# Cross network on one core: the first weights' queue, the products that start the clock, and a lag in the last layer's sums

## The chip, the cores and the metric

The kernel runs on one core of one Trainium2 chip. The metric is device time in microseconds (us) of one execution. A profile is one more execution, recorded by the hardware profiler; its "span" starts at the first instruction of the core, and all times of profiles below count from there.

The tables in plain fences below are worked out from the records of those traces (when each of the 16 DMA engines reported a landing, when a packet or an instruction started, when the granted TensorE clock changed).

## The reference

```python
B, F, D, L = 16384, 26, 16, 6
Din = min(F * D, 1024)                 # 416
def reference(x0, ws, bs):             # x0 (16384, 416), ws (6, 416, 416), bs (6, 416), bf16
    x = x0
    for l in range(6):
        proj = jnp.einsum('bd,de->be', x, ws[l]) + bs[l]
        x = x0 * proj + x
    return x
```

## The kernel before

The features lie on the partitions (three tiles of 128 and one of 32), the 16384 rows on the free axis, in eight groups of 2048 rows, a group in four chunks of 512. PE multiplies, ACT takes the products out of PSUM and adds the bias, DVE multiplies by x0 and adds x. Groups and layers are interleaved so that PE always has a tile to go on with. SP issues nearly all transfers.

The first group is loaded as rows and transposed on PE, the others by transposing transfers. The head of the program, with the transfers of the first group (`load_nat`), the first weights (`load_wm(0, ...)`) and the products that only keep PE busy:

```python
    load_wm(0, "act")                      # first weights, 312 KB, on ACT's queue
    load_nat(0, 0, 2)                      # first chunk of rows, first half, on SP's queue
    load_nat(0, 2, KK)                     # second half
    for j in range(1, NJ):
        load_nat(j, 0, KK)                 # chunks 2 to 4, 416 KB each
    load_w3(0, "sp")
    load_group(1, lambda: load_wm(1, "sp"))
    ...
    def keep_busy(n, b):
        for _ in range(n):
            add("pe", lambda h: h.matmul(bank(b, n=P), ident[:, :], ident[:, :], start=True, stop=True),
                reads=["ident"], writes=[("ps", b)])
    keep_busy(14, 7)
    ...
    def first_job():
        transposed_chunk(0)                # 16 transposes, with keep_busy(2, 3) after the sixth
        ...                                # the biases, transposed on PE
        keep_busy(8, 3)
        full(g, l, 0, ba, True, True, chunks=[0])   # first real products, 128x512
        full(g, l, 1, bb, True, True, chunks=[0])
        transposed_chunk(1)
        ...
```

The last layer of the last group is computed with the rows on the partitions, in four blocks `kk`, so that its result can be stored as it is. For each block DVE makes two products (`nat_mul`) and two sums (`nat_add`, which need rows that a transposing transfer has turned):

```python
    for j in (0, 2):
        nat_mul(0, j)
    for j in (0, 2):
        nat_add(0, j)
    nat_store(0, 0, NJ)
    ...                                    # block 1 and block 2 have this form:
    for j in range(NJ):
        nat_full(1, j, bks[1][j], False)   # PE
        nat_out(1, j, bks[1])              # ACT
        if j % 2:
            nat_mul(1, j - 1)              # DVE
            nat_add(1, j - 1)
    nat_store(1, 0, NJ)
    ...
    for j in range(NJ):                    # block 3, the last
        nat_full(kk, j, bks[kk][j], False)
        nat_out(kk, j, bks[kk])
        nat_mul(kk, j, 1)
        if j % 2:
            nat_add(kk, j - 1)
            nat_store(kk, j - 1, j + 1, "sp" if j == 1 else "act")
```

## Time and profile before

| | before |
|---|---|
| time, first three runs | 477.93 us median (477.69 to 478.12) |
| span of the profiled run | 474.6 us (time 476.43) |
| PE busy | 461.7 us, 97% |
| chain of work that ended last | PE 93% |

From the page of the kernel before (part 1, and the line by engine of part 4):

```profile
span 474.6 us, 8339 instructions
...
PE 461.7 (97%) x3317; PEld 195.3 (41%) x3371; DVE 403.7 (85%) x696; ACT 342.3 (72%) x372; POOL 6.3 (1%) x15
...
PE 93%; DVE 2%; ACT 2%; issue 1%; DMA 1%; POOL 0%; POOLq 0%; DVEq 0%
```

PE is the bound nearly everywhere. The change, though, touches only the two ends. The timeline of the first microseconds of the kernel before (start, duration, engine, line, operation, what it writes and reads, count; in brackets how long the engine had been idle and what ended that):

```profile
1.41 0.41 ACTq L280 DMA_DIRECT2D wm<-in_ws_dram  x1
1.43 0.29 POOL L510 TENSOR_SCALAR_AFFINE_SELECT ident<-ident 128x128 bf16<-128x128 bf16 x1 [0.23 <-POOL ident L509]
...
1.78 1.68 PE L541 MATMUL ps<-ident 128*128 128x128 bf16 x14 [1.78 <-POOL ident L510]
...
3.34 0.82 PE L561 MATMUL ps<-ident,x 128*128 128x128 bf16 x6
...
3.95 0.42 PE L541 MATMUL ps<-ident 128*128 128x128 bf16 x2
...
4.17 0.98 PE L561 MATMUL ps<-ident,x 128*128 128x128 bf16 x10
...
5.81 1.46 PE L456 MATMUL ps<-x,wm 128*128 128x512 bf16 x5
```

PE can start its opening products only when POOL has made the identity at 1.77 us. Fourteen of them take 1.68 us (107 ns from one to the next), and the first transposes follow at the same pace, because the TensorE clock is still at half speed; it rises at 4.70 us. The first real products (L456) start at 5.8 us.

The chain of waits of the same profile, cut to its first 24 us (start, duration, what):

```profile
1.78 1.68 PE ps L541 x14
3.46 0.71 PE ps L561 x6
...
5.42 0.55 PE ps L541 x8
5.97 0.43 PE ps L456 x2
...
21.75 0.54 PE ps L477 x8
```

The start hangs on POOL, then on PE and once on ACT. The last piece shown is the first use of the small rows (the 32 features left over) of the second group.

The tail, timeline of the kernel before (L858 are products, L864 sums, L871 the stores of the last group):

```profile
463.63 1.09 DVE L864 TENSOR_TENSOR x<-x,x 128x832 bf16<-128x832 bf16 x2 [0.56 <-DMA x<-x]
...
469.15 0.65 DVE L858 TENSOR_TENSOR x<-x,x 128x416 bf16<-128x416 bf16 x2
469.84 0.59 DVE L864 TENSOR_TENSOR x<-x,x 128x832 bf16<-128x832 bf16 x1
470.35 0.65 DVE L858 TENSOR_TENSOR x<-x,x 128x416 bf16<-128x416 bf16 x2
471.03 0.59 DVE L864 TENSOR_TENSOR x<-x,x 128x832 bf16<-128x832 bf16 x1
471.66 0.41 ACTq L871 DMA_DIRECT2D out_dram<-x  x1
```

and two of its last stretches (from:to, their length, busy time and instructions of PE, weight load, DVE, ACT and POOL, the granted clock, the busy share of the DMA engines, and what they moved, GB/s):

```profile
471.00:472.00 1.00, 0.00 (x0) 0.00 (x0) 0.59 (x1) 0.00 (x0) 0.00 (x0) 1.00 1.11 330
472.00:473.00 1.00, 0.00 (x0) 0.00 (x0) 0.00 (x0) 0.00 (x0) 0.00 (x0) 0.66 0.85 267
```

DVE works without a pause from 463.6 us, when the turned rows have come (`<-DMA x<-x`), to the last sum; the last store is issued at 471.66 us, while the queue still moves 330 GB/s. Only in the next microsecond does that fall, to 267 GB/s.

### The profile page before, as it was taken

How to read it: one execution, taken by the hardware profiler on the slowest of the kernel's cores; microseconds unless marked ns; L12 is line 12 of the kernel's file. 1: busy time of each engine (PE TensorE's matmuls, PEld its weight loads, DVE VectorE, ACT ScalarE, POOL GpSimd, SP SyncE). 2: the span in 40 equal slices, each digit the busy share in tenths (PEclk: the TensorE clock that was granted, in tenths of full speed). 3: DMA queues.
4: the chain of work that ended last, by engine and by line, in shares of the span. 5: the costliest groups of instructions: out<-in, count | busy, mean ns of one | idle time of the engine just before them, and what ended most of it. 6: DMA issues, size and time to landing. Idle time of an engine off the chain costs nothing.

```text
span 474.6 us, 8339 instructions
## 1 busy us (share of the span) xinstructions
PE 461.7 (97%) x3317; PEld 195.3 (41%) x3371; DVE 403.7 (85%) x696; ACT 342.3 (72%) x372; POOL 6.3 (1%) x15
## 2 busy tenths in 40 slices
PE   8999999999999999999999999999999999999995
PEld 6344444444444444444444444444444444444442
DVE  2888888888888888898889869988888888888896
ACT  4677777777777777777777777777777777777785
POOL 1000000000000000000000000000000000001000
PEclk9999999999999999999999999999999999999999
DMA  9876930750102377379219931980000039025999
GB/s 235 182 173 144 185 79 1 143 80 1 34 1 46 74 215 156 77 154 249 65 27 207 208 93 20 181 266 0 2 12 23 8 63 241 13 46 116 226 154 293
DMA packets 138364, 53.31 MB, mean 112 GB/s; under 512 B 112331, under 2 KB 137429, under 8 KB 138325
## 3 DMA queue, kind: packets, MB, share of 16 engines
q1 hardware_dynamic: 137448, 52.14, 48.9%
q10 hardware_dynamic: 876, 0.64, 0.4%
q8 instruction: 26, 0.43, 0.4%
q14 instruction: 14, 0.11, 0.1%
HBM read 5.97 MB, written 13.63 MB: 41 GB/s over the span
## 4 chain that ended last, share of the span: by engine, by line
PE 93%; DVE 2%; ACT 2%; issue 1%; DMA 1%; POOL 0%; POOLq 0%; DVEq 0%
PE ps L456 76%; PE ps L477 7%; PE ps L497 6%; ACT tw L394 1%; DMA x<-x 1%; PE ps L471 1%; DVE x L864 1%; PE ps L561 1%; DVE x L858 1%; PE ps L488 1%; PE ps L541 1%; DVE x L408 1%; DVE tw L403 0%; ACT x L565 0%; POOL ident L510 0%
## 5 line engine op out<-in xcount | busy, mean ns | idle before, releaser
L394 ACT ACTIVATE tw<-ps,bias 128x1024 bf16<-128x1024 f32 (+1 forms) x295 | 299.8, 1071 | 119.8 <-PE ps L477 74.4
L456 PE MATMUL ps<-x,wm 128*128 128x512 bf16 x1638 | 371.9, 379 | 5.6 <-issue 3.7
L456 PEld LDWEIGHTS ps<-x,wm 128*128 128x128 bf16 x1692 | 158.9, 98 | 213.3 <-issue 27.9
L403 DVE TENSOR_TENSOR tw<-tw,x 128x1024 bf16<-128x1024 bf16 (+1 forms) x285 | 192.4, 683 | 53.3 <-ACT tw L394 53.1
L408 DVE TENSOR_TENSOR x<-tw,x 128x1024 bf16<-128x1024 bf16 (+1 forms) x285 | 182.5, 680 | 0.0
L477 PE MATMUL ps<-x,w 32*128 32x512 bf16 x512 | 39.2, 379 | 0.0
L497 PE MATMUL ps<-x,wm 128*32 128x512 bf16 x564 | 33.0, 380 | 0.0
L434 ACT ACTIVATE ts<-ps,bias 128x512 bf16<-128x512 f32 x47 | 28.8, 701 | 0.0
L438 DVE TENSOR_TENSOR x<-ts,x 128x512 bf16<-128x512 bf16 x47 | 18.6, 416 | 3.4 <-DMA x<-x 3.4
L497 PEld LDWEIGHTS ps<-x,wm 128*32 128x32 bf16 x564 | 13.8, 96 | 17.6 <-issue 5.3
L477 PEld LDWEIGHTS ps<-x,w 32*128 32x128 bf16 x512 | 7.8, 92 | 27.6 <-issue 27.1
L436 DVE TENSOR_TENSOR ts<-ts,x 128x512 bf16<-128x512 bf16 x47 | 18.5, 416 | 0.0
L666 POOL COPY ost<-ot 128x512 bf16<-128x512 bf16 x6 | 4.9, 813 | 422.7 <-DMA ot<-x 422.7
L798 PE MATMUL ps<-wm,x 128*128 128x416 bf16 x48 | 9.5, 340 | 0.0
L852 ACT ACTIVATE x<-ps 128x416 bf16<-128x416 f32 x16 | 7.7, 533 | 2.0 <-PE ps L798 1.9
L568 DVE COPY x<-ps 128x512 bf16<-128x512 bf16 x4 | 1.7, 425 | 7.6 <-PE ps L561 7.6
L565 ACT ACTIVATE x<-ps 128x512 bf16<-128x512 bf16 x8 | 4.2, 598 | 4.6 <-PE ps L561 4.6
L798 PEld LDWEIGHTS ps<-wm,x 128*128 128x128 bf16 x48 | 4.3, 98 | 4.2 <-issue 1.0
L488 PE MATMUL ps<-x,w 32*32 32x512 bf16 x188 | 5.9, 374 | 0.0
L471 PE MATMUL ps<-x,w 32*32 32x512 bf16 x208 | 5.6, 385 | 0.0
L864 DVE TENSOR_TENSOR x<-x,x 128x832 bf16<-128x832 bf16 x8 | 4.6, 591 | 0.8 <-DMA x<-x 0.6
L858 DVE TENSOR_TENSOR x<-x,x 128x832 bf16<-128x832 bf16 (+1 forms) x10 | 4.8, 499 | 0.5 <-ACT x L852 0.5
(38 smaller groups left out, 35.0 us busy)
## 6 DMA issues: line engine op xcount, KB each, us to landing
out_dram<-ost SPq DMA_DIRECT2D x6, 1664.0 KB, 7.0
x<-in_x_dram SPq DMA_DIRECT2D x7, 416.0 KB, 7.9
x<-x SPq DMA_DIRECT2D x24, 96.0 KB, 2.2
out_dram<-ost SPq DMA_DIRECT2D x2, 832.0 KB, 6.9
wm<-in_ws_dram SPq DMA_DIRECT2D x5, 312.0 KB, 3.9
x<-x SPq DMA_DIRECT2D x22, 64.0 KB, 2.0
out_dram<-x SPq DMA_DIRECT2D x3, 416.0 KB, 4.5
x<-ost SPq DMA_DIRECT2D x28, 32.0 KB, 2.3
```

The lines of the kernel that those rows point to most:

```text
L394: add("act", lambda h, a=a, w=w, b0=b0: h.activation(tw[r][:, a * CH:(a + w) * CH], psum[:, b0 * CH:(b0 + w) * CH], ACT_F.Identity, bias=b ...
L403: add("dve", lambda h, a=a, e=e: h.tensor_tensor(tw[r][:, a * CH:e * CH], tw[r][:, a * CH:e * CH], x0s[s0][:, i * GC + a * CH:i * GC + e * ...
L408: add("dve", lambda h, a=a, e=e: h.tensor_tensor(xs[so][:, i * GC + a * CH:i * GC + e * CH], tw[r][:, a * CH:e * CH], src(i, a, e), ALU.ad ...
L434: add("act", lambda h: h.activation(ts[r][:, :], bank(b), ACT_F.Identity, bias=bias[:, 3, l:l + 1], scale=1.0), reads=[("ps", b), "bias"], ...
L436: add("dve", lambda h: h.tensor_tensor(ts[r][:, :], ts[r][:, :], x03, ALU.mult), reads=[("ts", r)] + tok0, writes=[("ts", r)], release=True)
L438: add("dve", lambda h: h.tensor_tensor(x3s[so][:, :], ts[r][:, :], res, ALU.add), reads=[("ts", r)] + rtok, writes=[("x3", so), ("x3", so, ...
L456: add("pe", lambda h, t=t, j=j: h.matmul(bank(banks[j]), wm[l][:, t, ecols], src(t, j, j + 1), start=(first and t == 0), stop=(not first a ...
L471: add("pe", lambda h, q=q, j=j, r=r, c=c, o=o: h.matmul(psum[o, banks[j] * CH:(banks[j] + 1) * CH], w3[l][q, i * P + c * T32:i * P + (c + ...
L477: add("pe", lambda h, q=q, j=j, r=r: h.matmul(bank(banks[j]), w3[l][q, ecols], src[q, :], start=first, stop=not first, tile_position=(r * ...
L488: add("pe", lambda h, l=l, b=b, s3=s3, ri=ri, qi=qi, ro=ro, qo=qo: h.matmul(psum[qo, b * CH:(b + 1) * CH], w3[l][qi, NT * P:D], s3[qi, :], ...
L497: add("pe", lambda h, t=t, j=j, src=src, l=l, b=b, ro=ro, qo=qo: h.matmul(psum[qo, b * CH:(b + 1) * CH], wm[l][:, t, NT * P:D], src(t, j, ...
L798: add("pe", lambda h, t=t: h.matmul(bank(b, n=D), xcol(t, j, kk), wm[l][:, t, :], start=(first and t == 0), stop=(not first and t == NT - 1)),
```

## The change

The intent has three parts. The first weights move from ACT's queue to SP's, behind the first chunk of rows, so that they do not take turns with those rows. The opening products use the matrix of ones, which is ready before the identity, so they can start sooner and there are 22 of them. And the sums of the last layer lag one product behind, so that DVE does a product where it would wait for a sum's operands.

```diff
-    load_wm(0, "act")
     load_nat(0, 0, 2)
     load_nat(0, 2, KK)
+    load_wm(0, "sp")
...
-            add("pe", lambda h: h.matmul(bank(b, n=P), ident[:, :], ident[:, :], start=True, stop=True),
-                reads=["ident"], writes=[("ps", b)])
-    keep_busy(14, 7)
+            add("pe", lambda h: h.matmul(bank(b, n=P), ones[:, :], ones[:, :], start=True, stop=True),
+                reads=["ones"], writes=[("ps", b)])
+    keep_busy(22, 7)
...
+    sums = []
+    def nat_sum():
+        kk, j = sums.pop(0)
+        nat_add(kk, j)
+        if kk == last:
+            nat_store(kk, j, j + 2, "sp" if j == 0 else "act")
+        elif j:
+            nat_store(kk, 0, NJ)
+    last = KK - 1
     for j in (0, 2):
         nat_mul(0, j)
-    for j in (0, 2):
-        nat_add(0, j)
-    nat_store(0, 0, NJ)
...                                        # blocks 1 to 3 as they were: taken out
+        sums.append((0, j))
+    nat_sum()
+    for kk in range(1, KK):
+        ...                                # nat_rows, nat_full, nat_out as before
+            if kk == last:
+                nat_mul(kk, j, 1)
+            elif j % 2:
+                nat_mul(kk, j - 1)
+            if j % 2:
+                sums.append((kk, j - 1))
+                nat_sum()
+                if kk == last and j == 1:
+                    nat_sum()
```

More of the change, by code (lines that the diff above doesn't have):

```diff
@@ L893, in bass_standalone__cross_network_dcn__recsys_kernel @@
     turned_out(2, b2)
+    sums = []
[7 more added lines that the diff above has]
+    last = KK - 1
     for j in (0, 2):
         nat_mul(0, j)
-    for j in (0, 2):
-        nat_add(0, j)
-    nat_store(0, 0, NJ)
-    nat_rows(1, bks[1])
-    for j in range(NJ):
-        nat_full(1, j, bks[1][j], False)
-        nat_out(1, j, bks[1])
-        if j % 2:
-            nat_mul(1, j - 1)
-            nat_add(1, j - 1)
-    nat_store(1, 0, NJ)
-    nat_rows(2, bks[2])
-    for j in range(NJ):
-        nat_full(2, j, bks[2][j], False)
-        nat_out(2, j, bks[2])
-        if j % 2:
-            nat_mul(2, j - 1)
-            nat_add(2, j - 1)
-    nat_store(2, 0, NJ)
-    kk = KK - 1
-    nat_rows(kk, bks[kk])
-    for j in range(NJ):
-        nat_full(kk, j, bks[kk][j], False)
-        nat_out(kk, j, bks[kk])
-        nat_mul(kk, j, 1)
-        if j % 2:
-            nat_add(kk, j - 1)
-            nat_store(kk, j - 1, j + 1, "sp" if j == 1 else "act")
+        sums.append((0, j))
+    nat_sum()
+    for kk in range(1, KK):
+        nat_rows(kk, bks[kk])
+        for j in range(NJ):
+            nat_full(kk, j, bks[kk][j], False)
+            nat_out(kk, j, bks[kk])
+            if kk == last:
[7 more added lines that the diff above has]
+                    nat_sum()
     pr.emit()
```

## The prediction

> **What bounds the kernel now.** The page: PE busy 461.7 of 474.6 us (97%); the chain of waits is 93% PE. The change touches only the first 6 us and the last 10 us; time can move only there.
>
> *Head (timeline, single instructions).* The first clock product starts at 1.78 us, when POOL has made the identity; products follow every 107 ns until about 4.65 us, every 56 ns after. The Trainium skill ("TensorE: Matmul & The Clock Gate", Part 1) gives 106.7 ns for the cold clock and 55.6 ns for the warm one; the trace agrees. The first rows land at 3.30 us, their transposes start at 3.34, the first real matmul at 5.81. The first weights, issued by ACT at 1.41 us, land at 5.24; their packets already run between those of the first rows and of the second chunk. DMA is busy almost without a break from 2 to 20 us. The second chunk lands at 6.77 (transposed from 7.11), the last small rows of the second group at 21.55, just before PE uses them at 21.68.
>
> *Tail (timeline, DMA packets).* The queue writes output without a break from 463 to 473.5 us, about 330 GB/s. The product/sum pairs on DVE run every 1.13 us (0.61 us from a product to its own sum, 0.51 otherwise). The last store is issued at 471.66; its packets start 0.94 us later and it lands at 474.11.
>
> **What the change does.**
> 1. Weights on SP's queue behind the first chunk: the same bytes in practically the same order; the skill ("DMA: Bandwidth & Descriptors", rules table) says that issuing from several engines gives no bandwidth. Expected: weights at 4.4 to 5.0 us instead of 5.24, later loads unchanged. Alone: 0.
> 2. Products of ones: ones are ready at 0.94 us, so products start at 1.0 instead of 1.78. 22 x 107 ns = 2.35 us: they still end as the rows land (3.35). The clock rises about 0.8 us sooner on average, so some ten transposes take 56 instead of 107 ns: first matmul near 5.5. The second chunk's landing cuts these 0.3 us to 0.2, the landing at 21.55 us to about 0.1: PE meets those rows earlier, but they come when they came. Estimate: -0.1 us (0 to -0.3).
> 3. Lagging sums: DVE loses the 0.1 us gap between a product and its own sum, but then waits for ACT's last copies, which come at PE's pace. At the end two sums stand before the last two products instead of one. Laid out with traced durations, the third block's store goes out at about 470.15 instead of 469.26, too late to follow when the queue runs dry (470.49, less 0.94 of latency), and the last store at about 471.85 instead of 471.66. Estimate: +0.2 us (-0.3 to +0.5).
>
> **Sum.** The two about cancel; as a lag is normally put in because it helps, I lean a little to faster: 477.8 us, 8 in 10 between 476.9 and 478.8. Chances: faster by over 2% 0.01, within 2% 0.98, slower 0.01.
>
> **What would show it.** First clock product at 1.0 us; 56 ns pitch from about 3.9; first 128x512 matmul near 5.5; PE waiting for the small rows near 21.6, everything after within 0.2 us of before. Tail: a gap in the write packets near 471; last landing 0.2 us later, counted from the last layer's first matmul.
>
> **What would make it wrong.** The second group's loads landing earlier (up to -0.5 us); the rows landing before the 22 products end; the clock window falling otherwise (its phase is not the kernel's), which moves single runs by 0.3 us.

## The result, and the profile after

| | before | after |
|---|---|---|
| time, six runs each in turn | 477.81 us median (476.62 to 479.89) | 477.48 us median (476.49 to 478.17) |
| span of the profiled run | 474.6 | 475.7 |

The ratio is 0.999, with a 95% interval from 0.9967 to 1.0014: the same. (A ratio is the mean time of one kernel's fast runs over that of the other's of the same rounds, so it is not quite the ratio of the medians quoted here.)

The timeline of the first microseconds of the kernel after:

```profile
0.99 2.53 PE L541 MATMUL ps<-ones 128*128 128x128 bf16 x22 [0.99 <-POOL ones L506]
...
1.65 0.43 SPq L280 DMA_DIRECT2D wm<-in_ws_dram  x1
...
3.31 0.76 PE L561 MATMUL ps<-ident,x 128*128 128x128 bf16 x6
...
3.90 0.28 PE L541 MATMUL ps<-ones 128*128 128x128 bf16 x2
...
4.01 0.72 PE L561 MATMUL ps<-ident,x 128*128 128x128 bf16 x10
...
5.57 0.99 PEld L456 LDWEIGHTS ps<-x,wm 128*128 128x128 bf16 x6 [0.18 <-ACT x L565]
...
7.92 1.07 PE L561 MATMUL ps<-ident,x 128*128 128x128 bf16 x16 [0.87 <-DMA x<-in_x_dram]
```

The products start at 0.99 us, as intended, and the clock rises at 3.84 us: the two products at 3.90 take 0.28 us for 0.42 before, the ten transposes 0.72 for 0.98. But after the first real products PE stands still for 0.87 us, until 7.92 us, for the second chunk of rows. The chain of waits of the kernel after says it more plainly:

```profile
2.13 5.75 DMA x<-in_x_dram
...
7.92 1.08 PE ps L561 x16
...
22.84 0.54 PE ps L477 x8
```

One transfer, issued at 2.13 us, holds the chain up to 7.88. The small rows of the second group are used 1.1 us later than in the profile of before. From there to the end the two profiles agree: 435.62 us from this use to the first product of the last layer in both (and within 0.02 us of that in all fourteen profiles). The whole program is therefore a head, a fixed middle and a tail, and only head and tail need to be compared.

The tail of the kernel after, timeline:

```profile
464.49 0.59 DVE L864 TENSOR_TENSOR x<-x,x 128x832 bf16<-128x832 bf16 x1 [0.32 <-DMA x<-x]
...
470.31 0.38 DVE L858 TENSOR_TENSOR x<-x,x 128x416 bf16<-128x416 bf16 x1 [0.15 <-ACT x L852]
470.60 1.09 DVE L864 TENSOR_TENSOR x<-x,x 128x832 bf16<-128x832 bf16 x2
471.61 0.66 DVE L858 TENSOR_TENSOR x<-x,x 128x416 bf16<-128x416 bf16 x2
472.30 0.59 DVE L864 TENSOR_TENSOR x<-x,x 128x832 bf16<-128x832 bf16 x1
472.92 0.42 ACTq L871 DMA_DIRECT2D out_dram<-x  x1
```

and the stretches that answer to those shown of before:

```profile
471.00:472.00 1.00, 0.00 (x0) 0.00 (x0) 1.00 (x4) 0.33 (x1) 0.00 (x0) 1.00 0.42 125
472.00:473.00 1.00, 0.00 (x0) 0.00 (x0) 0.85 (x2) 0.00 (x0) 0.00 (x0) 1.00 0.90 291
```

Two sums stand before the last two products (470.60 x2). In one microsecond the queue moves only 125 GB/s: it ran dry, as the third block's store came too late to follow. Counted from the first product of the last layer (457.30 and 458.39 us), the last store is issued at 14.53 us instead of 14.36, and lands at 16.81 in both.

So in this pair of profiles the head lost 1.1 us and the tail nothing, while the times say that the changed kernel is not slower. The pair misleads: the profiled run of before took 476.43 us, less than any of the 45 timed runs of that kernel (476.62 to 481.41). What one profile shows of the head is one draw.

### The profile page after: what moved, and what is told of

Read it like the earlier page. It is cut to its first block, busy times and chain, and to the rows that moved or that the text cites. A ratio compares the mean times of both kernels' runs of the same rounds, so it can differ in the third digit from the quotient of the medians.

```text
span 475.7 us, 8355 instructions
## 1 busy us (share of the span) xinstructions
PE 462.2 (97%) x3325; PEld 195.7 (41%) x3379; DVE 404.0 (85%) x696; ACT 342.4 (72%) x372; POOL 6.8 (1%) x15
## 4 chain that ended last, share of the span: by engine, by line
PE 95%; issue 1%; DMA 1%; ACT 1%; DVE 1%; SPq 0%
PE ps L456 77%; PE ps L477 7%; PE ps L497 6%; PE ps L798 2%; DMA x<-in_x_dram 1%; PE ps L471 1%; ACT tw L394 1%; PE ps L561 1%; PE ps L488 1%; DVE x L864 0%; PE ps L809 0%; ACT x L852 0%; DVE x L858 0%; PE ps L841 0%; SPq L521 0%
## 5 line engine op out<-in xcount | busy, mean ns | idle before, releaser
L852 ACT ACTIVATE x<-ps 128x416 bf16<-128x416 f32 x16 | 7.7, 533 | 2.0 <-PE ps L798 1.9
L561 PE MATMUL ps<-ident,x 128*128 128x128 bf16 x64 | 4.6, 226 | 1.4 <-DMA x<-in_x_dram 0.9
```

## The experiments

Each call ran four kernels in turn with the kernel before on one chip, five rounds each.

### First call: before again, and each part alone

`e1_before` is the kernel before. The others add one part of the change to it; `e1_weights`:

```diff
-    load_wm(0, "act")
     load_nat(0, 0, 2)
     load_nat(0, 2, KK)
+    load_wm(0, "sp")
```

`e1_clock` changes only `keep_busy` (ones, and 22), `e1_lag` only the end of the last layer; both as in the diff above.

> The kernel before, unchanged, a second time: how far the head moves by itself. In the first profile of before the second chunk of rows landed at 6.77 us and its transposes began at 7.11; in that of after 7.88 and 7.92. Theory C (chance: the loads stall for up to 1 us at places that change from run to run): the landing is somewhere from 6.5 to 8.0 us here too, and not tied to the kernel. Rival Q (queue: weights behind the first chunk on the same queue are fed more slowly than on a queue of their own): about 6.8 us again, as the weights are on ACT's queue here. Total: same as before, ratio 0.998 to 1.002.

> Only the first part: the first weights on SP's queue behind the first chunk, all else as before. Theory C: no change of the total (ratio 0.999 to 1.001), second chunk at 6.5 to 8.0 us by chance. Rival Q: between 3.2 and 4.4 us the queue moves only 70 to 100 KB in 0.4 us instead of 145, the weights land at about 5.4 and the second chunk at about 7.9 us, and the total is about 1 us longer (ratio 1.002).

> Only the second part: 22 products of ones instead of 14 of the identity, weights on ACT's queue, sums as before. Clock warm (56 ns pitch) at about 3.9 us, the first 128x512 matmul at 5.3 to 5.8. Theory C: PE then waits for the second chunk, which lands when it lands, so the gain is 0 to 0.3 us, ratio 0.999 to 1.000. Rival Q: the second chunk at about 6.8 us, the gain of 0.3 us is kept to that point, ratio about 0.999; with the weights on SP's queue it would be hidden by the later chunk.

> Only the third part: the lagging sums. Head as in before. From the first matmul of the last layer to the last landing 16.8 us in the first profile of before. My theory: the third block's store goes out 0.9 us later, a gap of about 0.4 us opens in the write packets before it, the last store goes out 0.2 us later; from that first matmul to the end +0.0 to +0.3 us. Rival (the lag frees the vector engine from waiting for the turned rows, which is what it is for): -0.3 us or more. Total ratio 0.999 to 1.001 either way.

(Six runs of each kernel count here and in the later calls, five of `e1_weights`; 11 of before in each call.)

| | median us | range | ratio to before, 95% interval |
|---|---|---|---|
| before, in turn | 477.79 | 476.80 to 481.41 | |
| e1_before | 477.93 | 477.23 to 478.38 | 1.0001 (0.9983 to 1.0019) |
| e1_weights | 477.33 | 477.04 to 477.78 | 0.9991 (0.9971 to 1.0010) |
| e1_clock | 477.14 | 476.66 to 479.65 | 0.9994 (0.9968 to 1.0019) |
| e1_lag | 477.39 | 476.89 to 479.66 | 1.0000 (0.9977 to 1.0022) |

No part can be told from nothing by its time. The profiles tell more. In the second profile of the unchanged kernel the chain of waits runs through a transfer too, and through another one:

```profile
1.40 5.47 DMA wm<-in_ws_dram
...
7.01 0.59 PE ps L456 x2
...
22.95 0.54 PE ps L477 x8
```

Here the first weights are late (6.88 us, 5.24 in the first profile), PE starts the real products at 7.01 instead of 5.81, and the second group's rows are used 1.2 us later than in the first profile: as late as in the profile of after, with nothing changed. Which transfer is late differs; how it is late is seen in the landings of its 16 DMA engines one by one (us):

```
kernel      transfer       first  ...  8th   ...  14th  15th  16th
before      first weights  4.39        4.62       4.73  5.05  5.24
e1_before   first weights  4.41        4.57       4.74  4.78  6.88
e1_weights  first weights  4.60        5.14       5.61  5.68  6.00
after       first weights  4.47        5.12       5.41  5.42  5.46
before      second chunk   5.48        5.67       6.34  6.64  6.77
e1_before   second chunk   5.46        5.60       5.77  5.81  6.38
after       second chunk   5.80        6.27       6.50  6.51  7.88
```

The Trainium skill ("DMA: Bandwidth & Descriptors", "Why a DMA increments its semaphore by 16 and not by 1") says that a DMA's engines finish independently and that only the full count means that all data landed. Fifteen of sixteen parts of the weights were there at 4.78 us, and PE waited until 6.88 for the sixteenth.

Theory C (chance) is borne out for what PE waits for: the last engine's landing of the second chunk was 6.38, 7.34, 7.67 and 7.29 us in these four profiles (6.38 is a little under the range expected), with no relation to the queue; over all fourteen the ranges overlap, 6.38 to 7.67 with the weights on ACT's queue and 6.55 to 8.25 with them on SP's behind the first chunk. The microsecond that rival Q expected for `e1_weights` (ratio 1.002) lies outside its interval. Rival Q is right on a smaller matter: the bulk does come later on SP's queue (8th engine of the weights at 5.1 us against 4.6 on ACT's). In `e1_clock` the clock rose at 6.16 us and the first real weight load came at 6.28; both were expected sooner (3.9, and products at 5.3 to 5.8).

The profile of `e1_lag`, which has the head of before, shows a third kind of loss:

```profile
4.65 1.25 PE L561 MATMUL ps<-ident,x 128*128 128x128 bf16 x10 [0.29 <-DMA x<-in_x_dram]
...
6.12 1.03 PE L541 MATMUL ps<-ident 128*128 128x128 bf16 x8
...
8.23 1.49 PE L456 MATMUL ps<-x,wm 128*128 128x512 bf16 x3 [0.22 <-issue]
```

The second half of the first rows came at 4.60 us, PE stood still for 0.29 us, and from then on everything is at half speed: eight products take 1.03 us for 0.62 before, and the weight loads of the real products come 427 ns apart (7.38, 7.80, 8.23) and not 216. The clock rose at 10.42 us; the second group's rows were used at 24.52, the latest of all profiles; that run took 479.66 us.

Why so late? The Trainium skill ("TensorE: Matmul & The Clock Gate", Part 1) says that the clock follows PE's activity in a free-running window of 3413 ns, which does not start with the kernel. The traces agree: the full-speed stretches last 464.21, 467.63 or 471.04 us, which is 136, 137 or 138 times 3.413. So the windows can be laid over each profile, backward from the rise, and for each the share of time in which PE streamed columns can be worked out (128 columns in 107 ns at the slow clock, as traced; another way of counting moves a share by about a point):

```
kernel      first   window that raised   windows before it that did
            product the clock            not raise it, with PE's share
before      1.78    1.29 to 4.70   84%   -
e1_before   1.78    1.36 to 4.77   83%   -
e1_weights  1.77    1.63 to 5.04   93%   -
e1_clock    0.99    2.75 to 6.16   88%   up to 2.75  52%
e1_lag      1.78    7.01 to 10.42  88%   0.18 to 3.59  52%,  3.59 to 7.01  74%
after       0.99    0.42 to 3.84   83%   -
```

A window with 83% or more raised the clock, one with 74% or less did not. The start of the products therefore decides only which window is the first to be full enough; where the windows lie is drawn anew in each run. And a pause at a bad place can spoil a window and cost a whole further one.

For the tail, all four kernels could be read from their profiles, counted from the first product of the last layer:

```
kernel      lag  turned rows landed  last store issued  it landed
before      0    6.22                14.36              16.81
e1_before   0    6.90                15.05              17.13
e1_weights  0    6.73                14.88              17.31
e1_clock    0    6.27                14.43              16.89
after       1    5.98                14.53              16.81
e1_lag      1    6.67                14.52              17.24
```

Without the lag the last store goes out 8.14 to 8.16 us after the turned rows have landed, whenever that is: DVE never catches up. With the lag it goes out at 14.52 to 14.53, whenever the rows land, because DVE then waits for ACT (`<-ACT x L852` in the tail of after), which follows PE. So both theories of the lag were half right: it does free DVE from the turned rows, and its own order costs 0.2 us against a run with rows at the usual time. The two are equal when the rows land at about 6.37 us (14.52 less 8.15); over all profiles they landed from 5.69 to 6.90, and after 6.37 in only three of fourteen, all of them in this first call (whether the chip or chance does that is not shown).

The end follows the last store only loosely: from its issue to its landing the table has 2.08 to 2.72 us. `e1_lag` has no gap before the third block, though one was expected: its write packets had paused for 1.27 us earlier in the tail, so the queue was still behind. In the mean the last landing is at 16.89 us in the six profiles without lag and at 16.93 in the six with a lag of one.

### Second call: the head alone, and each suspect made larger

`e2_head` is the changed kernel with the sums as before. The others change one thing in the changed kernel. `e2_noclock`:

```diff
-    keep_busy(22, 7)
```

`e2_wlate` (weights behind the second chunk) and `e2_lag2` (a lag of two products):

```diff
+    load_nat(1, 0, KK)
     load_wm(0, "sp")
-    for j in range(1, NJ):
+    for j in range(2, NJ):
```

```diff
         sums.append((0, j))
-    nat_sum()
...
-                if kk == last and j == 1:
+                while kk == last and sums:
                     nat_sum()
```

> Weights and clock parts, sums as before: the changed kernel without the lag, and the candidate for a better one. If the lag costs what I laid out (0.2 us), ratio to before 0.998 to 0.999 and from the last layer's first matmul to the last landing the same as before (16.8 to 17.3 us in three kernels without lag). Window theory W (the clock rises only at a boundary of windows of 3.413 us, and only if PE was busy over some 80% of the one that ended; the phase is new in every run): products from 0.99 us, so it rises between 3.8 and 7.2 us.

> The changed kernel without its 22 opening products (the 10 later ones stay). W: PE starts at 3.3 us with the first transposes, so the clock rises between 6.1 and 9.5 us or a window later, the first real matmuls run at half speed (427 ns), and the total is 1 to 2.5 us longer than the changed kernel's (ratio to before 1.001 to 1.004). Rival D (the head is paced by the loads alone, so the clock does not matter): within 0.5 us of the changed kernel, ratio 0.998 to 1.000.

> The changed kernel with the weights behind the second chunk instead of the first. If the weights' landing is the gate of the first real matmul (as in the second profile of before, 6.88 and 7.01 us): weights land at 6.3 to 7.2 us, the second chunk about 0.9 us sooner (5.5 to 6.8), the first 128x512 matmul 0.1 us after the weights, and the second group's rows are used 15.9 us after that; total +0.5 to +1.2 us against the changed kernel. Rival D: the total is the same, as the bytes up to the second chunk are.

> The changed kernel with the sums lagging two products instead of one: the lag's cost, doubled. My layout of the tail: three sums stand before the last two products, the third block's store goes out about 0.5 us later than with one lag and the last store too, so from the last layer's first matmul to the last landing about 17.3 us (one lag: 16.81 in the profile of after), and a gap of about 0.9 us in the write packets before the third block. Rival (the lag is free because the queue is behind anyway): no gap and the end unmoved.

| | median us | range | ratio to before, 95% interval |
|---|---|---|---|
| before, in turn | 477.60 | 476.89 to 479.99 | |
| e2_head | 477.13 | 476.63 to 477.45 | 0.9978 (0.9956 to 0.9999) |
| e2_noclock | 477.96 | 477.72 to 479.05 | 1.0003 (0.9982 to 1.0023) |
| e2_wlate | 477.83 | 477.39 to 478.29 | 0.9996 (0.9976 to 1.0016) |
| e2_lag2 | 477.79 | 477.19 to 478.43 | 0.9995 (0.9975 to 1.0016) |

Without the opening products, timeline of `e2_noclock`:

```profile
5.61 1.03 PE L541 MATMUL ps<-ones 128*128 128x128 bf16 x8
...
6.44 2.74 PE L456 MATMUL ps<-x,wm 128*128 128x512 bf16 x6
```

The six real products take 2.74 us (1.46 in before): the clock rose at 9.02 us, after a window with a share of 56% that did not raise it. The mean of its six runs is 478.19 us, 0.9 above the changed kernel's over its twelve (477.27; 95% interval of the difference about 0.3 to 1.5, and the twelve come from other calls), a little under the 1 to 2.5 that I expected. Rival D, for which the clock does not matter, wanted at most 0.5: the times speak against it without shutting it out, the slow products of the profile do so more plainly.

With the weights behind the second chunk, timeline of `e2_wlate`:

```profile
7.66 1.46 PE L456 MATMUL ps<-x,wm 128*128 128x512 bf16 x6 [0.98 <-DMA wm<-in_ws_dram]
```

They land at 7.52 us (expected 6.3 to 7.2), the second chunk at 6.09, and the products start 0.14 us after the weights, for which PE had waited 0.98 us. The mean, 477.86 us, is 0.6 above the changed kernel's (about 0.1 to 1.0). The first weights are a gate, too.

With a lag of two, the last store goes out at 15.03 us from the last layer's first product (14.53 with one), and lands at 17.31: half a microsecond for the second product of lag, as laid out (the first had cost the last store 0.2). The write packets have gaps of 0.32 us before the second block and 0.60 before the third (0.9 in all, as expected); both are seen in the stretches of `e2_lag2`:

```profile
469.00:470.00 1.00, 1.00 (x8) 0.49 (x5) 0.84 (x3) 0.98 (x3) 0.00 (x0) 1.00 0.64 189
...
471.00:472.00 1.00, 0.00 (x0) 0.00 (x0) 1.00 (x4) 0.00 (x0) 0.00 (x0) 1.00 0.46 155
```

Here the queue has no backlog left, so a later store is a later end.

`e2_head` came out a little better than expected: its last landing is at 16.62 us from the last layer's first product (16.8 to 17.3 expected), as its turned rows landed early, at 6.00; its clock rose at 6.41, in the expected range.

### Third call: the same pair again, a shorter lag, and products for too long

`e3_after` and `e3_head` are the changed kernel and `e2_head` again. `e3_clock44` has `keep_busy(44, 7)`. `e3_flush` ends the lag with the third block:

```diff
             if kk == last:
+                if j == 0:
+                    nat_sum()
                 nat_mul(kk, j, 1)
...
                 nat_sum()
-                if kk == last and j == 1:
-                    nat_sum()
```

> The changed kernel, unchanged, beside the other three on one chip. Median 477.2 to 477.8 us, ratio to before 0.998 to 1.000. In its profile the last store goes out 14.53 us after the last layer's first matmul whenever the turned rows have landed by about 6.6 us from there (14.52 to 14.53 in four kernels with one lag).

> The changed kernel without the lag, again, beside the changed kernel. If its first ratio (0.9978, interval 0.9956 to 0.9999) was real, it is 0.2 to 0.5 us faster than the changed kernel; if the lag is neutral on average, within 0.3 us of it. In its profile the last store goes out 8.15 us after the landing of the turned rows (8.14 to 8.16 in five kernels without lag), whatever that landing is.

> The changed kernel, but the lag ends with the third block: its last sum stands before the first product of the fourth, so one sum and not two stands between the products of the fourth. By the traced durations the third block's store goes out at about 12.0 us from the last layer's first matmul (12.83 with the lag) and the last at 14.36 (14.53), with no gap in the write packets before the third block, and both are independent of the turned rows' landing up to about 6.5 us. Total 0.0 to 0.3 us under the changed kernel: too little to be seen in the times, visible in the profile.

> The changed kernel with 44 opening products instead of 22: they keep PE from the first rows until 4.8 to 5.7 us. If the first real matmul hangs on PE and the clock as much as on the loads, it moves to 6.4 to 7.3 us and the total is 0.4 to 1.0 us longer than the changed kernel's. Rival D (the head is paced by the loads alone, PE has 1 us or more to spare): no longer than the changed kernel, within 0.3 us.

| | median us | range | ratio to before, 95% interval |
|---|---|---|---|
| before, in turn | 477.95 | 476.85 to 480.79 | |
| e3_after | 477.16 | 476.42 to 477.55 | 0.9980 (0.9959 to 1.0001) |
| e3_head | 476.53 | 476.21 to 477.64 | 0.9971 (0.9950 to 0.9992) |
| e3_flush | 477.12 | 476.48 to 478.13 | 0.9982 (0.9958 to 1.0005) |
| e3_clock44 | 477.66 | 477.34 to 478.41 | 0.9993 (0.9973 to 1.0014) |

`e3_clock44`, timeline:

```profile
0.99 4.51 PE L541 MATMUL ps<-ones 128*128 128x128 bf16 x44 [0.99 <-POOL ones L506]
...
7.16 1.46 PE L456 MATMUL ps<-x,wm 128*128 128x512 bf16 x6
```

The products push the first real ones to 7.16 us, and the mean of its runs is 477.73 us, 0.6 above the changed kernel of the same call (477.09; 95% interval of the difference about 0.1 to 1.2). PE has no microsecond to spare in the head of this profile, and this speaks against rival D (at most 0.3) as well: by the profiles the head hangs on the clock, on PE and on the loads, whichever is last in that run.

`e3_flush`, tail of the timeline:

```profile
470.03 0.66 DVE L858 TENSOR_TENSOR x<-x,x 128x416 bf16<-128x416 bf16 x2
470.72 0.59 DVE L864 TENSOR_TENSOR x<-x,x 128x832 bf16<-128x832 bf16 x1
471.23 0.66 DVE L858 TENSOR_TENSOR x<-x,x 128x416 bf16<-128x416 bf16 x2
...
472.54 0.42 ACTq L871 DMA_DIRECT2D out_dram<-x  x1
```

One sum (470.72) stands between the last two pairs of products. The last store goes out at 14.31 us from the last layer's first product and lands at 16.57, for 14.52 and 16.80 in the profile of `e3_after` of the same call; there is no dry stretch. The order of stores is as laid out. `e3_head` has the same end here (14.15, 16.60), as its rows were early (5.99). None of these 0.2 us shows in the times of `e3_flush`.

Over all calls, which ran on different chips, the changed kernel without the lag took 476.87 us in the mean of 12 runs, the changed kernel 477.27 of 12, before 477.99 of 45 (the runs of before in turn with all four results, and `e1_before`). The medians of the same runs are 476.73, 477.41 and 477.89: the mean of before holds a few long runs. `e3_head` and `e2_head` are the best seen: 0.2 to 0.3% under before, with both intervals just clear of 1, and 0.4 us under the changed kernel, where the scatter of a single run is 0.5 (95% interval of this difference about 0.0 to 0.8 over all twelve runs of each, -0.2 to 1.0 in the third call alone).

### All heads side by side

The gates of all profiles (us; "rows used" is the first use of the second group's small rows, after which all profiles are alike; all columns but the second, fifth and last are the landing of a transfer's last engine):

```
kernel      clock  weights  second  first real    second group's  rows
            rises           chunk   weight load   rows landed     used
before       4.70   5.24    6.77     5.76         21.55           21.68
e1_before    4.77   6.88    6.38     6.98         21.96           22.88
e1_lag      10.42   6.39    7.29     6.84         22.36           24.52
e1_weights   5.04   6.00    7.34     6.11         21.61           22.00
e1_clock     6.16   5.25    7.67     6.28         22.31           22.35
e2_head      6.41   6.89    8.25     6.99         22.89           22.93
e3_head      4.38   5.47    6.55     5.60         22.08           22.12
after        3.84   5.46    7.88     5.57         22.53           22.77
e3_after     3.93   6.29    7.52     6.40         22.05           22.29
e3_flush     7.00   6.06    7.64     6.38         22.25           22.61
e2_lag2      5.70   5.47    6.96     6.07         22.23           22.27
e2_noclock   9.02   5.46    6.58     6.33         22.71           23.59
e2_wlate     6.51   7.52    6.09     7.63         22.26           23.52
e3_clock44   4.96   5.95    6.98     7.11         22.58           23.02
```

In six of them (`before`, `e1_before`, `e1_weights`, `e3_after`, `e2_wlate`, `e3_clock44`) the rows are used 15.9 us after the first real weight load, and not because they had just landed: that is PE's own work from there. In four (`e1_clock`, `e2_head`, `e3_head`, `e2_lag2`) they are used 0.04 us after they landed: the loads (in `e2_head` PE's own work ended at the same time, 15.94 us after its first real weight load). In `e1_lag`, `e2_noclock` and `e3_flush` the clock rose only after the first real products had begun, and the way is 1.8, 1.4 and 0.3 us longer; in `after` the second chunk makes it 1.3 us longer.

The further windows agree with the share found above: 38, 59, 62 and 56% (`e2_lag2`, `e2_head`, `e2_wlate`, `e2_noclock`) did not raise the clock, nor did 76% in `e3_flush`; 84, 88, 99 and 100% did. The limit lies between 76 and 83%.

## Why the prediction was right or wrong

The forecast of the total, 477.8 us and no change at 2%, held: 477.48 us. Its steps:

- *Products from 1.0 us, clock at about 3.9, ten transposes at 56 ns*: as forecast in the profile of after (0.99, 3.84), partly by luck, as the place of the window is drawn in each run. But the rise was 6.16, 6.41 or 7.00 us in other profiles with the same start. The forecast knew that the phase is drawn and called it 0.3 us; the size was wrong. A window that is missed costs a further 3.4 us at half speed, and in `e1_lag` the rows were used 1.6 us later than in `e1_before`, most of it for that.
- *Weights alone: 0, landing at 4.4 to 5.0 us*: the landing was wrong. The bulk came later on SP's queue (8th engine at 4.8 to 5.3 instead of 4.6 us), and the last engine at 5.46 to 6.89 in the nine profiles with the weights on SP's queue behind the first chunk (5.24 to 6.88 in four on ACT's). So the first real products, forecast near 5.5 us, had to wait about 0.2 us for them in the profile of after (5.46, first weight load 5.57; its line names ACT, whose copy ended at 5.52, but the load follows the weights by 0.11 us, as it does in the five profiles whose weights came clearly last). That the part alone gives nothing is neither shown nor refuted: ratio 0.9991, interval 0.9971 to 1.0010.
- *The head's gain is cut to 0.1 us, as the second group's rows land at 21.55 us*: this is the term that was mis-sized. By the times the two head parts together are worth about 1.1 us (476.87 against 477.99 in the mean, from the intervals of the ratios 0.05 to 2.1 us in one call and 0.4 to 2.4 in the other). The profiles show the direction and not the size: the rows are used at 22.5 us in the mean of the six profiles with exactly both head parts, at 23.0 in the three with the head of before, and these three lie 2.8 us apart. Which of the two parts brings the gain is not shown. The cap exists (four profiles of fourteen), but it had been read from a profile in which those rows landed earlier than in any other. Rows used near 21.6 us and everything after within 0.2 us of before, which was to show this step right, was not what the profile of after had: 22.77, as its second chunk was late. The head of before that was costed was the best of three, not the usual one.
- *Lag: the third block's store 0.9 us later, a gap near 471 us, the last store 0.2 us later*: all three as laid out (12.83 for 11.97, the dry stretch, 14.53 for 14.36). The end itself did not move in that pair (16.81 both). In the times the lag costs 0.4 us (477.27 against 476.87, interval about 0.0 to 0.8), forecast 0.2; the profiles have 0.2 in the pair of the third call (16.80 against 16.60) and 0.04 in the mean of all. So its size stays open, between nothing and some tenths.
- *The sum*: -0.1 forecast, -0.7 in the means of all runs (477.27 against 477.99), -0.3 in the medians of the first result. The head's gain was forecast at a tenth of what the times show; the total is right all the same because its two terms together are small against the range of the forecast (476.9 to 478.8). That is partly luck.

What stays open: why one of 16 engines comes a microsecond or two after the others; and whether the weights on SP's queue prevent slow runs. Of the runs with the weights on ACT's queue 8 of 57 took over 479 us, of those with the weights on SP's queue 1 of 59. A way for that is seen once (in `e1_lag` the second half of the first rows landed at 4.60 us, at most 4.09 in every profile with the weights behind it, and a window was spoiled), but in the three other profiles with ACT's queue it landed by 3.90: one profile does not show it.

## What to carry to other kernels

When a change is worth a few tenths of a microsecond, one profile of each kernel cannot be compared: take the landing times and clock of several profiles of the same kernel first, and cost the change against the usual one, not against the one at hand. Products that only wake the clock are worth having from the first instant that any operand exists, but only as many as end when the data comes: none cost about 0.9 us here and twice as many about 0.6. A lag in a consumer's order frees it from a late operand and delays the stores behind it; by the profile of `e3_flush` it is better ended before the last block, though the times do not show it.

## What the Trainium skill lacked or had wrong

- "TensorE: Matmul & The Clock Gate", Part 1, asks for a busy window of about 3.4 us and does not say how busy. Here windows with a streaming share of 83% and more raised the clock and those with 76% and less did not (14 profiles, shares to about a point); a pause of 0.29 us was part of one that failed with 74%, and the clock then rose at 10.42 us.
- The same page, Part 4, says that a PE transpose does not count as busy in the way that a product does and that the full clock does not engage for it. Here transposes counted: the window of `e1_clock` that raised the clock (2.75 to 6.16 us) was 88% full with them and 37% without, while 68% of plain products and 8% of transposes did not raise it in `e3_flush`. Transposes after the rise came every 56 ns, as products did.
- "DMA: Bandwidth & Descriptors" says that the issuing engine makes no difference to bandwidth. No run here contradicts that, but the landing did change: the 8th of 16 engines had the same weights at 4.6 us on ACT's queue and at 4.8 to 5.3 on SP's behind the first chunk. Queue and place were changed together, and the issue went from 1.41 to 1.65 us, so which of them did it is not shown.
- No page gives the size of the spread between the engines of one transfer: here the last of 16 came up to 2.1 us after the 15th (first weights of `e1_before`), and the first real products came 1.2 us later than in the other profile of the same kernel.
